# Attention with a sixth of the exp tiles taken from ScalarE to VectorE, heads regrouped by four, and the order set by a planner

## Chip, cores and metric

One core of a Trainium2 chip runs the kernel. The metric is device time in microseconds (us) of one execution, lower is better; medians are over the runs quoted.

## The reference

The block is a sum of an attention and a feed-forward part on the same normalised input, 2048 positions of width 640:

```python
xn = layernorm(x)                                   # x: [1, 2048, 640] bf16
q  = (xn @ wq) split in 32 heads of 20 columns
k, v = xn @ wk, xn @ wv                             # one k and v for all heads
p  = softmax(q k^T / sqrt(20));  o = p v
h  = relu(xn @ w1 + b1) ** 2                        # 1536 wide
out = x + o @ wo + h @ w2 + b2
```

The exp of the scores decides everything: 32 x 2048 x 2048 values. On the chip a tile of them is 128 keys by 512 queries of one head, so there are 2048 tiles (16 key tiles, 4 query chunks, 32 heads).

## The kernel before

Scores are made by TensorE (QK) into two alternating sets of three banks of PSUM (the memory that matmuls write to), one bank for each head of a group of three. ScalarE turns one set into bf16 probabilities with a single exp instruction, and TensorE multiplies them with the values (P-V), accumulating in one bank. Head groups are ten of three and one of two. Everything else on TensorE (query projections, feed-forward, output projection) is cut into small pieces and put between these steps, and where nothing is left, **fillers** are: matmuls with all-zero weights that add 0 to the open P-V sum.

```python
for j in range(NSTEP):                       # 704 steps, cut to the core
    for i in range(HPG):                     # HPG = 3, one bank for each head
        matmul(ps[:, 3*(j%2)+i, :], kT[32*i:32*i+DH, ...], qT[32*i:32*i+DH, ...])   # QK, waits for exp j-2
    activation(out=PT[:, j % NSLOT, 0:nh, :], in_=ps[:, sset:sset+nh, :], func=Exp) # one exp, 2 or 3 banks
    ...
    nfill = 0
    if CFG["enable_fill"] and pvs:
        while busy + COL_NS <= CFG["fill_target_ns"] - (1344.0 - step_ns) + COL_NS / 2:
            nfill += 1                       # fill_target_ns = 1060 of a 1344 ns step
            busy += COL_NS
    emit_pv(k, nfill)                        # fillers, then P-V of an earlier step
    ...
def fillers(k, nh):
    for _ in range(k):
        for jj in range(4):                  # four column groups run together
            matmul(ps[32*jj:32*jj+32, PVB, :], zeros32, kT[:, 0:512], start=False, stop=False)
```

Five dummy matmuls stand ahead of the first QK step. And GpSimd (POOL) clears the pad of the output projection only after the second QK step:

```python
memset(wo_pad, 0.0), waits=[(st_done, 2)]    # on POOL
```

The softmax here doesn't subtract the row's maximum and nothing guards it: scores larger than these inputs give would overflow.

Of the kernel before, what the change touches and what calls it, by code (L numbers as in the profile page):

```python
# [6 lines left out]
F32 = mybir.dt.float32  # L7
ALU = mybir.AluOpType
# [4 lines left out]
HPG = 3  # L13
G = (H + HPG - 1) // HPG
NSLOT = 6
NQS = 4


def NH(g):
    return min(HPG, H - HPG * g)  # L20


GORDER = [0, 1, 2, 3, 4, G - 1, 5, 6, 7, 8, 9]
assert sorted(GORDER) == list(range(G))
SHORT_GI = GORDER.index(G - 1)


def BLK(b):
    qc, gi = divmod(b, G)
    return qc, gi, GORDER[gi]  # L30

SCALE = DH ** -0.5
EPS = 1e-5
NBLK = QC * G
NSTEP = NBLK * KT
# [3 lines left out]
CFG = dict(  # L39
    misc_budget_ns=620.0,  # L40
    fill_target_ns=1060.0,
    enable_fill=True,
    warm_n=22,
    sched_trials=400,
    npro=3,
    npkv=2,
    act_slot_wait=False,
    pre_loop_dummies=5,
    short_fill=1,
    pro_fill=6,  # L50
)
ROW4_NS, COLF_NS, COL_NS, COL320_NS = 390.0, 320.0, 206.0, 140.0
PRO_SCHED = []
# [45 lines left out]

def bass_parallel_sum__grouped_kv_mqa__dense_activation_squared_relu__prompt_kernel(nc, A_x, A_wq, A_wk, A_wv, A_wo, B_x, B_w1, B_b1, B_w2, B_b2, out):  # L100
    es = ExitStack()
    with es:  # L102
# [22 lines left out]
        vx = sb("vx", [128, KT, 32], BF16)  # L125
        qT = sb("qT", [128, NQS, 512], BF16)
        PT = sb("PT", [128, NSLOT, HPG, 512], BF16)
# [11 lines left out]
        out_sb = sb("out_sb", [128, 4, D], BF16)  # L139
        part = sb("part", [128, 4, D], F32)  # L140
        zeros32 = sb("zeros32", [128, 32], BF16)
        scr = sb("scr", [128, 4], F32)
        nk0 = sb("nk0", [128, 2], F32)
        ps = es.enter_context(nc.psum_tensor("ps", [128, 8, 512], F32))

        PVB = 6
        MB = 7
# [4 lines left out]
        junk_src = [PT[:, k, :, :].rearrange("p a n -> p (a n)")[:, 0:D] for k in range(NSLOT)] + \  # L152
# [18 lines left out]
        osem = [newctr(f"osem{i}") for i in range(4)]  # L171
        c_pool = newctr("c_pool")
# [13 lines left out]
        misc_pe = newctr("misc_pe")  # L186
        misc_free = newctr("misc_free")
        act_done = newctr("act_done")
        st_done = newctr("st_done")
        pv_done = newctr("pv_done")  # L190
        pv_evac = newctr("pv_evac")
        c_nrm = newctr("c_nrm")
        norm_done = newctr("norm_done")
        sq_done = newctr("sq_done")
        c_aux = newctr("c_aux")
        c_k0 = newctr("c_k0")

        P = Plan()

        class Unit:  # L200
            def __init__(self, name, groups, n, pe_waits, evac, bank=MB, kind="mm", ncol=4, need_norm=0):
                self.name = name
                self.ncol = ncol
                self.need_norm = need_norm
                self.groups = groups
                self.n = n
                self.pe_waits = pe_waits
                self.evac = evac
                self.bank = bank
                self.kind = kind  # L210
                self.idx = None
                self.next_group = 0
                self.v_done = None

            def cost(self):
                return (COL_NS if self.n >= 500 else COL320_NS)

        unit_seq = []
        last_unit_in_bank = {}

        def emit_unit_group(u):
            k = u.next_group
            L, R = u.groups[k]
            last = (k == len(u.groups) - 1)
            bank = u.bank
            for j in range(u.ncol):
                w = []
                if k == 0 and j == 0:
                    u.idx = len(unit_seq)
                    unit_seq.append(u)  # L230
                    w = list(u.pe_waits() if callable(u.pe_waits) else u.pe_waits)
                    if bank in last_unit_in_bank:
                        w.append((misc_free, last_unit_in_bank[bank] + 1))
                    last_unit_in_bank[bank] = u.idx
                inc = misc_pe if (last and j == u.ncol - 1) else None
                if callable(L):
                    Lj = L(j)
                    m = DH
                else:
                    Lj = L[:, 32 * j:32 * j + 32]  # L240
                    m = 32
                add(P.pe, lambda e, j=j, Lj=Lj, R=R, k=k, last=last, n=u.n, bank=bank, m=m: e.matmul(  # L242
                    ps[32 * j:32 * j + m, bank, 0:n], Lj, R, start=(k == 0), stop=last, tile_position=(0, 32 * j)),
                    waits=w, inc=inc)
            u.next_group += 1
            if last:
                u.v_done = misc_pe.n
                assert u.v_done == u.idx + 1
                u.evac(u)
            return last  # L250

        def emit_unit_all(u):
            while not emit_unit_group(u):
                pass

        qt_units = {}

        def unit_QT(b):
            qc, gi, g = BLK(b)
            groups = [((lambda j, dt=dt: wq_sb[:, dt, DH * (HPG * g + j):DH * (HPG * g + j) + DH]), xnT[:, dt, qc * 512:(qc + 1) * 512]) for dt in range(DT)]  # L260
            pe_waits = [te_wait(st) for st in range(4 * qc, 4 * qc + 4)] + [(wq_sem, 16)]

            def evac(u):
                w = [(misc_pe, u.v_done)]
                if b >= NQS:
                    w.append((st_done, KT * (b - NQS + 1)))
                add(P.dve, lambda e: e.tensor_copy(out=qT[:, b % NQS, :], in_=ps[:, u.bank, :]), waits=w, inc=misc_free)  # L267
            u = Unit(f"QT{b}", groups, 512, pe_waits, evac, ncol=NH(g))
            qt_units[b] = u
            return u  # L270

        ffn_count = [0]
        last_out_unit_of_qc = {}

        def unit_FFN1(qc, f):
            groups = [(w1_sb[:, dt, f * 128:(f + 1) * 128], xnT[:, dt, qc * 512:(qc + 1) * 512]) for dt in range(DT)]
            pe_waits = [te_wait(st) for st in range(4 * qc, 4 * qc + 4)] + [(w1_sem, 16)]

            def evac(u):
                k = ffn_count[0]  # L280
                ffn_count[0] += 1
                w = [(misc_pe, u.v_done), (misc_free, b1_unit[0].idx + 1)]
                if k >= 2:
                    w.append((sq_done, k - 1))
                v_relu = add(P.dve, lambda e: e.tensor_scalar(out=hT_tmp[:, k % 2, :], in0=ps[:, u.bank, :], scalar1=b1col[:, f:f + 1], scalar2=0.0,  # L285
                                                              op0=ALU.add, op1=ALU.max), waits=w, inc=misc_free)
                w2 = [(misc_free, v_relu)]
                if qc >= 2:
                    w2.append((misc_pe, last_out_unit_of_qc[qc - 2]))
                add(P.pool, lambda e: e.tensor_tensor(out=h2T[:, qc % 2, f, :], in0=hT_tmp[:, k % 2, :], in1=hT_tmp[:, k % 2, :], op=ALU.mult),  # L290
                    waits=w2, inc=sq_done)
            return Unit(f"FFN{qc}_{f}", groups, 512, pe_waits, evac)

        b1_unit = [None]

        def unit_B1():
            u = Unit("B1", [None], 0, [(b1_sem, 16), (c_pool, v_ident)], None, kind="b1")
            b1_unit[0] = u
            return u

        def emit_b1_unit(u):
            u.idx = len(unit_seq)
            unit_seq.append(u)
            w = list(u.pe_waits() if callable(u.pe_waits) else u.pe_waits)
            if MB in last_unit_in_bank:
                w.append((misc_free, last_unit_in_bank[MB] + 1))
            last_unit_in_bank[MB] = u.idx
            add(P.pe, lambda e: e.transpose(out=psbf(MB)[:, 0:FT], in_=b1row[:, :], identity=ident[0:FT, 0:FT]), waits=w, inc=misc_pe)
            u.next_group = 1
            u.v_done = misc_pe.n  # L310
            add(P.dve, lambda e: e.tensor_copy(out=b1col[:], in_=psbf(MB)[:, 0:FT]), waits=[(misc_pe, u.v_done)], inc=misc_free)
            return True

        out_dma_count = [0, 0, 0, 0]
        GP1 = 7

        def out_groups(qc, st, half, gs, with_ffn):
            stl = st % 4
            cs = slice(half * 320, half * 320 + 320)
            groups = []  # L320
            if with_ffn:
                for f in range(FT):
                    groups.append((h2T[:, qc % 2, f, stl * 128:(stl + 1) * 128], w2_sb[:, f, cs]))
# [685 lines left out]
```

## Time and profile before

The median was 961.25 us of 3 runs (960.55 to 969.2). The first fence has lines of the profile's page: busy time by engine; busy tenths of ScalarE (ACT) and the granted TensorE clock (PEclk, tenths of full speed) in 40 equal slices of the span; the chain of work that ended last; and two of the costliest groups (busy us, mean ns of one | idle before it).

```profile
span 955.9 us, 26306 instructions
...
PE 851.0 (89%) x12183; PEld 287.5 (30%) x12184; DVE 205.6 (22%) x382; ACT 938.5 (98%) x750; POOL 65.5 (7%) x71
...
ACT  7999999999999999999999999999999999999995
...
PEclk8999999999999999999999999999999999999998
...
ACT 94%; PE 3%; DVE 2%; DMA 1%; issue 0%; ACTq 0%; SPq 0%; DVEq 0%
...
L891 ACT ACTIVATE PT<-ps 128x1536 bf16<-128x1536 f32 (+1 forms) x704 | 918.9, 1767 | 1.4 <-PE ps L888 1.2
...
L814 PE MATMUL ps<-kT,zeros 128*32 128x512 bf16 x2316 | 183.9, 385 | 0.0
```

ScalarE is the bound: 98% busy, 94% of the chain, and the exp group was idle for 1.4 us in all. TensorE (PE) looks busy too (89%), but 183.9 us of that is fillers. The clock is at full speed from start to end. VectorE (DVE) works 22% of the time, so moving exp work there is natural. The second fence is the grouping by shape, which gives the price of an exp instruction: 861.7/640 = 1.346 us for three banks.

```profile
L891 ACT ACTIVATE PT<-ps 128x1536 bf16<-128x1536 f32 x640 | 861.7, 1819 | 1.4 <-PE ps L888 1.2
...
L891 ACT ACTIVATE PT<-ps 128x1024 bf16<-128x1024 f32 x64 | 60.5, 1255 | 0.0
```

In a two-head stretch of the timeline exp instructions follow each other every 0.917 us. So one instruction costs about 0.06 us plus 0.43 us for each 512-column tile. The third fence has busy time in three stretches of 60 us (columns: stretch, length, busy us and instruction count of PE, PEld, DVE, ACT and POOL, then the granted clock, DMA share, GB/s).

```profile
core 0: us, PE busy (x) PEld busy (x) DVE busy (x) ACT busy (x) POOL busy (x), PEclk, DMA share, GB/s
60.00:120.00 60.00, 52.23 (x675) 15.07 (x667) 10.45 (x18) 60.00 (x46) 2.08 (x2) 1.00 0.01 1
180.00:240.00 60.00, 52.08 (x680) 15.05 (x672) 9.18 (x17) 60.00 (x46) 2.08 (x2) 1.00 0.01 2
270.00:330.00 60.00, 54.23 (x836) 19.28 (x832) 11.52 (x20) 60.00 (x46) 2.08 (x2) 1.00 0.01 4
```

### The profile page before, as it was taken

To read this page: it belongs to the slowest core of one execution; us is meant where nothing else is said; L and a number is where in the kernel's file an instruction comes from. 1 tells how busy PE (TensorE), PEld (TensorE's weight loads), DVE (VectorE), ACT (ScalarE), POOL (GpSimd) and SP (SyncE) were. 2 spreads that over 40 slices of the span, in tenths; PEclk is the share of its full clock that TensorE was granted. 3 is DMA by queue.
4 is the path that set the end of the run, shared out by engine and by line. 5 is a ranking of instruction groups with operands and counts; after the bars stand their busy time and mean duration, and the time that the engine had idled before them with its cause. 6 is when DMAs were issued, how large, how long until landed. Compare 5 with 4: busy or idle time off the path is not lost.

```text
span 955.9 us, 26306 instructions
## 1 busy us (share of the span) xinstructions
PE 851.0 (89%) x12183; PEld 287.5 (30%) x12184; DVE 205.6 (22%) x382; ACT 938.5 (98%) x750; POOL 65.5 (7%) x71
## 2 busy tenths in 40 slices
PE   6988889888899998998888998999889999999996
PEld 3322222222233332332233332333223333233332
DVE  6312211112211211211111112121113222112214
ACT  7999999999999999999999999999999999999995
POOL 4300000000000000000000000010001111000000
PEclk8999999999999999999999999999999999999998
DMA  9100000000000000000000000000000000000000
GB/s 311 37 2 1 1 1 1 2 2 1 2 2 8 9 2 1 9 2 8 1 2 9 2 8 2 8 2 9 2 1 2 9 2 8 2 9 2 9 2 29
DMA packets 9412, 12.54 MB, mean 13 GB/s; under 512 B 1751, under 2 KB 8664, under 8 KB 9304
## 3 DMA queue, kind: packets, MB, share of 16 engines
q1 hardware_dynamic: 7992, 10.82, 3.4%
q8 instruction: 96, 1.57, 0.7%
q10 hardware_dynamic: 1312, 0.05, 0.1%
q14 instruction: 12, 0.10, 0.0%
HBM read 8.25 MB, written 2.62 MB: 11 GB/s over the span
## 4 chain that ended last, share of the span: by engine, by line
ACT 94%; PE 3%; DVE 2%; DMA 1%; issue 0%; ACTq 0%; SPq 0%; DVEq 0%
ACT PT L891 94%; PE ps L888 1%; PE ps L242 1%; DMA x_sb<-in_A_x_dram 1%; PE ps L859 1%; PE ps L814 0%; PE ps L521 0%; DVE stats L438 0%; DVE out_sb L379 0%; PE ps L492 0%; DVE big L478 0%; DVE qT L267 0%; ACTq L102 0%; PE ps L529 0%; PE ps L431 0%
## 5 line engine op out<-in xcount | busy, mean ns | idle before, releaser
L891 ACT ACTIVATE PT<-ps 128x1536 bf16<-128x1536 f32 (+1 forms) x704 | 918.9, 1767 | 1.4 <-PE ps L888 1.2
L888 PE MATMUL ps<-qT,kT 20*128 20x512 bf16 x2112 | 275.3, 384 | 66.4 <-ACT PT L891 59.7
L859 PE MATMUL ps<-PT,vx 128*32 128x512 bf16 x2816 | 270.9, 384 | 1.2 <-ACT PT L891 1.2
L814 PE MATMUL ps<-kT,zeros 128*32 128x512 bf16 x2316 | 183.9, 385 | 0.0
L888 PEld LDWEIGHTS ps<-qT,kT 20*128 20x128 bf16 x2112 | 68.4, 90 | 362.6 <-ACT PT L891 349.6
L824 DVE STREAM_TRANSPOSE Tn<-ps 128x512 f32<-128x512 f32 x44 | 31.5, 717 | 449.0 <-PE ps L859 449.0
L859 PEld LDWEIGHTS ps<-PT,vx 128*32 128x32 bf16 x2816 | 70.3, 95 | 108.1 <-issue 77.3
L290 POOL TENSOR_TENSOR big<-hT_tmp 128x512 bf16<-128x512 bf16 x48 | 49.9, 1041 | 716.1 <-DVE hT_tmp L285 716.1
L242 PE MATMUL ps<-w_sb,big 128*32 128x320 bf16 x1536 | 69.1, 300 | 10.8 <-DVE qT L267 9.6
L242 PE MATMUL ps<-xnT,w_sb 128*32 128x512 bf16 x960 | 68.9, 380 | 9.8 <-DVE qT L267 7.6
L242 PE MATMUL ps<-wo_pad,OTn 128*32 128x320 bf16 x1408 | 65.5, 303 | 2.6 <-DVE part L365 2.6
L242 PE MATMUL ps<-xnT,wq_sb 128*20 128x512 bf16 x640 | 62.3, 379 | 1.8 <-DVE qT L267 1.8
L814 PEld LDWEIGHTS ps<-kT,zeros 128*32 128x32 bf16 x2316 | 37.7, 94 | 71.6 <-issue 71.6
L285 DVE TENSOR_SCALAR hT_tmp<-ps,b1col 128x512 bf16<-128x512 f32 x48 | 36.0, 750 | 87.7 <-PE ps L242 87.7
L242 PEld LDWEIGHTS ps<-w_sb,big 128*32 128x32 bf16 x1536 | 39.7, 96 | 32.6 <-issue 18.9
L242 PEld LDWEIGHTS ps<-wo_pad,OTn 128*32 128x32 bf16 x1408 | 38.0, 98 | 18.6 <-DVE OTn L839 2.9
L342 DVE TENSOR_TENSOR out_sb<-ps,x_sb 128x320 bf16<-128x320 f32 x24 | 11.8, 491 | 143.6 <-PE ps L242 143.6
L242 PEld LDWEIGHTS ps<-xnT,w_sb 128*32 128x32 bf16 x960 | 22.7, 95 | 32.7 <-issue 17.2
L267 DVE CAST qT<-ps 128x512 bf16<-128x512 f32 x44 | 29.0, 659 | 12.8 <-PE ps L242 12.8
L839 DVE STREAM_TRANSPOSE OTn<-T 128x512 bf16<-128x512 bf16 x44 | 31.1, 707 | 0.8
L831 DVE TENSOR_TENSOR T<-Tn 96x512 bf16<-96x512 f32 (+1 forms) x44 | 30.2, 687 | 1.5
L242 PEld LDWEIGHTS ps<-xnT,wq_sb 128*20 128x20 bf16 x640 | 21.0, 91 | 18.2 <-issue 2.2
(71 smaller groups left out, 135.0 us busy)
## 6 DMA issues: line engine op xcount, KB each, us to landing
w_sb<-in_B_w_dram SPq DMA_DIRECT2D x2, 1920.0 KB, 10.6
out_dram<-out_sb SPq DMA_DIRECT2D x16, 160.0 KB, 1.8
x_sb<-in_A_x_dram SPq DMA_DIRECT2D x3, 640.0 KB, 7.2
wq_sb<-in_A_wq_dram SPq DMA_DIRECT2D x1, 800.0 KB, 10.1
x_sb<-in_A_x_dram SPq DMA_DIRECT2D x2, 320.0 KB, 3.6
wo_pad<-in_A_wo_dram SPq DMA_DIRECT2D x2, 275.0 KB
wo_pad<-in_A_wo_dram SPq DMA_DIRECT2D x1, 250.0 KB
wk_c<-in_A_wk_dram ACTq DMA_DIRECT2D x1, 25.0 KB, 3.4
```

The source lines that it names most:

```text
L242: add(P.pe, lambda e, j=j, Lj=Lj, R=R, k=k, last=last, n=u.n, bank=bank, m=m: e.matmul(ps[32 * j:32 * j + m, bank, 0:n], Lj, R, start=(k = ...
L267: add(P.dve, lambda e: e.tensor_copy(out=qT[:, b % NQS, :], in_=ps[:, u.bank, :]), waits=w, inc=misc_free)
L285: v_relu = add(P.dve, lambda e: e.tensor_scalar(out=hT_tmp[:, k % 2, :], in0=ps[:, u.bank, :], scalar1=b1col[:, f:f + 1], scalar2=0.0, op0 ...
L290: add(P.pool, lambda e: e.tensor_tensor(out=h2T[:, qc % 2, f, :], in0=hT_tmp[:, k % 2, :], in1=hT_tmp[:, k % 2, :], op=ALU.mult), waits=w2 ...
L342: v = add(P.dve, lambda e: e.tensor_tensor(out=out_sb[:, slot, cs], in0=ps[:, u.bank, 0:320], in1=x_sb[:, st, cs], op=ALU.add), waits=w, i ...
L814: add(P.pe, lambda e, jj=jj: e.matmul(ps[32 * jj:32 * jj + 32, PVB, :], zeros32[:, :], kT[:, 0:512], start=False, stop=False, tile_positio ...
L824: add(P.dve, lambda e: e.transpose(out=Tn[:, a, :], in_=ps[:, PVB, :]), waits=w, inc=pv_evac)
L831: st8["v2"] = add(P.dve, lambda e: e.tensor_tensor(out=T2[0:pp, a, :].rearrange("p (c d) -> p c d", d=32), in0=Tn[0:pp, a, :].rearrange("p ...
L839: add(P.dve, lambda e: e.transpose(out=OTn[:, qc % 2, g, :], in_=T2[:, a, :]), waits=w3, inc=norm_done)
L859: add(P.pe, lambda e, i=i, t=t, hs=hs: e.matmul(ps[32 * i:32 * i + 32, PVB, :], vx[:, t, :], PT[:, j % NSLOT, hs, :], start=(t == 0), stop ...
L888: add(P.pe, lambda e, i=i, t=t, b=b, sset=sset: e.matmul(ps[:, sset + i, :], kT[32 * i:32 * i + DH, t * 128:(t + 1) * 128], qT[32 * i:32 * ...
L891: add(P.act, lambda e, j=j, nh=nh, sset=sset: e.activation(out=PT[:, j % NSLOT, 0:nh, :], in_=ps[:, sset:sset + nh, :], func=AF.Exp, bias= ...
```

## The change

Its intent: give 84 of the 512 (head group, query chunk, key tile) sets of four tiles to VectorE, so that ScalarE has 1712 tiles instead of 2048. VectorE has to build the exp from bit patterns. One step scales the score and writes it as a 16-bit integer: read as bf16, these bits `L` are 2^e times a mantissa u in [1, 2). Two mask steps give `W` (the exponent with a constant mantissa) and `U` = u; two multiplies give `T` = L u u. TensorE then sums three P-V products with the values scaled by 1, 0.5 and 0.164, which is 2^e (u + 0.98 + 0.164 u^3), close to a constant times 2^e 2^u. One bank is VectorE's; ScalarE keeps two sets, of three and of two banks. The second multiply of every other set runs on POOL.

Heads are in 8 groups of four, so P-V and normalisation passes drop from 44 to 32. The order of all instructions comes from a list scheduler in the kernel that has a duration for each instruction and puts the real work of each engine into its free time. The fillers are gone. So are the five dummies and the wait of the memset. The diff, cut to its core (marked ...):

```diff
-HPG = 3
-G = (H + HPG - 1) // HPG
+HPG = 4
+G = H // HPG
...
+ACT_BANKS = ((0, 1, 2), (3, 4))
+DBANKS = (5,)
+T2POOL = (0, 1)
...
-            add(P.pool, lambda e: e.memset(wo_pad[:], 0.0), waits=[(st_done, 2)], inc=c_pool)
+            add(P.pool, lambda e: e.memset(wo_pad[:], 0.0), waits=[], inc=c_pool)
...
-        pe_dummies(CFG["pre_loop_dummies"])
-        for j in range(NSTEP):
...          # and the fillers, with all of the fixed step loop
+            d1 = dv(... e.tensor_scalar(out=lbuf[:, a, cs].bitcast(U16), in0=ps[:, bank, :], scalar1=XA, scalar2=XB, op0=ALU.mult, op1=ALU.add) ...)
+            s["wop"] = [dv(... e.tensor_scalar(out=W.bitcast(U16), in0=L.bitcast(U16), scalar1=0xFF80, scalar2=124, op0=ALU.bitwise_and, op1=ALU.bitwise_or) ...)]
+            s["uop"] = dv(... e.tensor_scalar(out=ubuf.bitcast(U16), in0=L.bitcast(U16), scalar1=0x7F, scalar2=0x3F80, op0=ALU.bitwise_and, op1=ALU.bitwise_or) ...)
+            s["t1"] = [dv(... e.tensor_tensor(out=T, in0=L, in1=ubuf, op=ALU.mult) ...)]
+            # second multiply: two halves on POOL in every other set, else on VectorE
+        while True:            # the planner: of all engines' ready work, take what can start first
...
```

## The prediction

It was written before the changed kernel had run.

> **What bounds it now.** ScalarE's exp. The page gives ACT 98% busy (938.5 of a 955.9 us span); the chain of waits puts 94% of the span on the exp line, and the exp group was idle only 1.4 us. By shape: 640 activations of 128x1536 (861.7 us, so 1.346 us each at full rate) and 64 of 128x1024; in a two-head stretch of the timeline one starts every 0.917 us. That is about 0.06 us per instruction plus 0.43 us per 512-column tile, 2048 tiles. About 37 us lie outside (first exp at 26.5 us; an 11 us tail). PE is 89% busy, but 184 us of that is filler matmuls on zeros; DVE only 22%, POOL 7%.
>
> **What the change does, by counted instructions.** 84 of 512 (block, key tile) sets, 336 of 2048 tiles, leave ScalarE. It keeps 1712 tiles in 342 three-tile and 343 two-tile steps: 342 x 1.344 + 343 x 0.917 = 774 us instead of 919. Gain 145 us.
>
> DVE gains, for each set: four PSUM-to-integer steps (128x512 from PSUM took 0.66 to 0.75 us in this trace), two mask operations on 128x2048 16-bit, one multiply, and in half of the sets a second multiply. The trace has none of the big ones; the Trainium skill, "VectorE: DVE Perf Modes", section "Side-by-side: where the cycles go for N=2048 bf16", gives about 0.69 us in 4x mode and 1.22 us in 2x (nothing here shows it yet). Estimate: 336 x 0.70 + 168 x 0.69 + 84 x 1.22 + 42 x 1.22 = 505 us. Groups of four need 32 instead of 44 normalisations and query casts (-35 us). DVE: about 675 us, over 80% of the new span. POOL gains 84 multiplies of 1024 columns, about 2.08 us each (twice its 512-column 1.041 us): +175 us.
>
> PE loses all 2316 fillers and a quarter of the P-V passes, gains 336 x 3 matmuls for the three terms. Estimate from strides in the timeline (0.32 us a QK step, 0.22 us four P-V columns): about 570 us, not the bound.
>
> **Critical path.** If exp stays saturated: 961 - 145 = 816 us. I do not expect that. DVE is now near full, in order, with one PSUM bank for its score tiles, whose matmul stands in PE's queue between ScalarE's QK steps: when DVE is late, PE blocks and ScalarE starves. DVE's two-port and two-input operations and POOL's multiplies exclude each other (Trainium skill, "SBUF — State Buffer", section "SBUF: two separate sides": an exclusive lock), so a 2.1 us POOL multiply can hold DVE. I allow 4 to 5% of stalls, about 35 us.
>
> **Predicted: 850 us, 8 in 10 between 824 and 892.** Faster by over 2%: 0.93; within 2%: 0.03; slower: 0.04.
>
> **What would show it.** Exp busy about 775 us, ACT 91 to 95% of the span, with 30 to 50 us idle released by PE's QK, behind PE waits on DVE's PSUM step. DVE near 80%, mask operations near 0.69 us, multiplies near 1.2 us, POOL multiplies near 2.1 us. PE near 70%, clock above 0.97.
>
> **What would make it wrong.** Mask operations not in 4x mode (1x would be over 2 us, +250 us on DVE: about 950 us or worse); lock waits that stretch DVE or POOL multiplies well beyond their durations; a PE clock that drops without fillers; or stalls under 1% (about 822 us).

## The result

The changed kernel took 884.65 us in the median of 4 runs (881.98 to 886.22), in the same job the kernel before 960.9. The ratio is 0.9188 (95% interval 0.9139 to 0.9238). Ratios here are the mean time of one kernel's fast runs over that of the other's in the same rounds, so they are not quite the ratios of the medians. It is faster, within the predicted range, but 35 us slower than the number predicted, and 69 us above the 816 us of a saturated ScalarE. Its page, with the lines that answer to those of before:

```profile
span 882.4 us, 20648 instructions
...
PE 790.4 (90%) x9319; PEld 239.7 (27%) x9319; DVE 658.4 (75%) x942; ACT 809.1 (92%) x732; POOL 251.3 (28%) x162
...
ACT  7599998998889999999889989999998999999895
...
PEclk8689987655569999977559999986576999965799
...
PE 48%; ACT 42%; DVE 6%; issue 1%; DVEq 0%
...
L840 ACT ACTIVATE PT<-ps 128x1536 bf16<-128x1536 f32 (+1 forms) x685 | 788.6, 1265 | 57.1 <-PE ps L533 54.0
...
L956 DVE TENSOR_SCALAR x_sb<-ps 128x512 uint16<-128x512 f32 x336 | 230.5, 686 | 140.8 <-PE ps L533 138.8
L972 POOL TENSOR_TENSOR tbuf<-tbuf,x_sb 128x1024 bf16<-128x1024 bf16 x84 | 178.8, 2151 | 435.5 <-DVE tbuf L967 435.5
...
L967 DVE TENSOR_TENSOR tbuf<-x_sb 128x2048 bf16<-128x2048 bf16 x84 | 103.7, 1235 | 1.4
...
L963 DVE TENSOR_SCALAR x_sb<-x_sb 128x2048 uint16<-128x2048 uint16 x84 | 69.3, 825 | 1.4
L965 DVE TENSOR_SCALAR x_sb<-x_sb 128x2048 uint16<-128x2048 uint16 x84 | 62.1, 740 | 0.0
```

Two things stand out. First, PEclk: 6 and 5 stand in long rows where before all were 9, and the mean clock is 0.814 (before 0.993). Second, the chain is now split between PE (48%) and ACT (42%), and exp waited 57.1 us, 54.0 of it for PE. VectorE's steps cost about what was foreseen: 0.686 us for a score tile, 1.235 us for a multiply, 0.74 and 0.825 us for the masks, 2.15 us for POOL's half multiply. The same three stretches as before:

```profile
core 0: us, PE busy (x) PEld busy (x) DVE busy (x) ACT busy (x) POOL busy (x), PEclk, DMA share, GB/s
60.00:120.00 60.00, 54.65 (x686) 16.01 (x690) 52.81 (x73) 59.44 (x53) 22.93 (x17) 1.00 0.01 2
180.00:240.00 60.00, 54.86 (x376) 10.97 (x376) 39.95 (x54) 51.59 (x45) 13.02 (x8) 0.53 0.00 1
270.00:330.00 60.00, 57.60 (x924) 21.69 (x924) 53.84 (x73) 59.72 (x54) 17.38 (x11) 1.00 0.06 18
```

At full clock (first and third row) ScalarE is busy 59.4 and 59.7 of 60 us and finishes 53 and 54 exp steps. At a clock of 0.53 it finishes 45. The lines of the timeline there, and of the same time in the kernel before (start, length, instructions), show why:

```profile
200.37 0.62 PE L533 MATMUL ps<-PT,vx 128*32 128x512 bf16 x4
200.77 1.07 PE L533 MATMUL ps<-xnT,w_sb 128*32 128x512 bf16 x8
...
204.14 0.61 PE L533 MATMUL ps<-qT,kT 20*128 20x512 bf16 x3
204.68 0.62 PE L533 MATMUL ps<-PT,vx 128*32 128x512 bf16 x4
```

```profile
201.40 0.39 PE L859 MATMUL ps<-PT,vx 128*32 128x512 bf16 x4
201.98 0.39 PE L888 MATMUL ps<-qT,kT 20*128 20x512 bf16 x3 [0.19 <-ACT PT L891]
202.30 0.61 PE L814 MATMUL ps<-kT,zeros 128*32 128x512 bf16 x8
```

Starts count here, since ends overlap. In the changed kernel four P-V matmuls take 0.40 us (200.37 to 200.77) and a QK step of three matmuls 0.54 (204.14 to 204.68). Before, a QK step of three took 0.32 (201.98 to 202.30), and in a full-clock stretch of the changed kernel four P-V matmuls take 0.22 (271.04 to 271.26). At about half speed PE can no longer refill the banks in the time of an exp: from 200 to 210 us PE was busy for 10.00 of 10 us, and exp was idle for 2.8 us waiting for it.

The start is also later. In the kernel before, the first exp began at 26.5 us; now at 31.4 us (the first line is of the kernel before, the second of the changed one):

```profile
26.54 2.97 ACT L891 ACTIVATE PT<-ps 128x1536 bf16<-128x1536 f32 x2 [1.01 <-PE ps L888]
```

```profile
31.44 2.37 ACT L840 ACTIVATE PT<-ps 128x1536 bf16<-128x1536 f32 x2 [5.38 <-PE ps L533]
```

The timeline of VectorE and POOL in the changed kernel:

```profile
23.46 5.97 DVE L301 TENSOR_SCALAR big<-x_sb,rstd,nmr 128x640 bf16<-128x640 bf16 x3
```

```profile
24.52 4.36 POOL L391 MEMSET wo_pad<- 128x5120 bf16 x1
```

Three normalising steps took 5.97 us together; one of them, by the per-tile view, 5.234 us, where the others took about 0.45. POOL ran a normalising step of its own from 23.53 (1.05 us) and right after it the memset, which lost its wait in the change, from 24.52 to 28.88. The long VectorE step spans both.

### The profile page after: what moved, and what is told of

Read it like the earlier page. It is cut to its first block, busy times and chain, and to the rows that moved or that the text cites. A ratio compares the mean times of both kernels' runs of the same rounds, so it can differ in the third digit from the quotient of the medians.

```text
span 882.4 us, 20648 instructions
## 1 busy us (share of the span) xinstructions
PE 790.4 (90%) x9319; PEld 239.7 (27%) x9319; DVE 658.4 (75%) x942; ACT 809.1 (92%) x732; POOL 251.3 (28%) x162
## 4 chain that ended last, share of the span: by engine, by line
PE 48%; ACT 42%; DVE 6%; issue 1%; DVEq 0%
PE ps L533 48%; ACT PT L840 42%; DVE x_sb L956 1%; DVE hT_tmp L652 1%; DVE Tn L890 1%; DVE qT L635 1%; DVE T L892 0%; DVE x_sb L965 0%; PE ps L581 0%; DVE out_sb L715 0%; DVE out_sb L1132 0%; DVE x_sb L963 0%; DVE part L734 0%; DVE OTn L896 0%; DVE tbuf L967 0%
## 5 line engine op out<-in xcount | busy, mean ns | idle before, releaser
L840 ACT ACTIVATE PT<-ps 128x1536 bf16<-128x1536 f32 (+1 forms) x685 | 788.6, 1265 | 57.1 <-PE ps L533 54.0
L533 PE MATMUL ps<-qT,kT 20*128 20x512 bf16 x2048 | 332.9, 458 | 63.2 <-ACT PT L840 55.2
L956 DVE TENSOR_SCALAR x_sb<-ps 128x512 uint16<-128x512 f32 x336 | 230.5, 686 | 140.8 <-PE ps L533 138.8
L972 POOL TENSOR_TENSOR tbuf<-tbuf,x_sb 128x1024 bf16<-128x1024 bf16 x84 | 178.8, 2151 | 435.5 <-DVE tbuf L967 435.5
L533 PE MATMUL ps<-PT,vx 128*32 128x512 bf16 x1712 | 201.6, 462 | 2.4 <-DVE Tn L890 2.4
L967 DVE TENSOR_TENSOR tbuf<-x_sb 128x2048 bf16<-128x2048 bf16 x84 | 103.7, 1235 | 1.4
L963 DVE TENSOR_SCALAR x_sb<-x_sb 128x2048 uint16<-128x2048 uint16 x84 | 69.3, 825 | 1.4
L965 DVE TENSOR_SCALAR x_sb<-x_sb 128x2048 uint16<-128x2048 uint16 x84 | 62.1, 740 | 0.0
L974 DVE TENSOR_TENSOR tbuf<-tbuf,x_sb 128x2048 bf16<-128x2048 bf16 x42 | 51.7, 1232 | 0.2
L533 PE MATMUL ps<-tbuf,vxc 128*32 128x512 bf16 x336 | 39.2, 456 | 0.3 <-POOL tbuf L972 0.2
L533 PE MATMUL ps<-x_sb,vxh 128*32 128x512 bf16 x336 | 38.8, 452 | 0.0
```

The lines of the kernel that those rows point to most:

```text
L533: return lambda e: e.matmul(out_, l, r, start=start, stop=stop, tile_position=tp)
L840: return Op(f"ACT{st_['j']}", "ACT", 0.064 + 0.4267 * n, [lambda e: e.activation(out=PT[:, s0:s0 + n, :], in_=ps[:, b0:b0 + n, :], func=AF ...
L956: d1 = dv(f"D1_{n}_{i}", 0.66, lambda e: e.tensor_scalar(out=lbuf[:, a, cs].bitcast(U16), in0=ps[:, bank, :], scalar1=XA, scalar2=XB, op0= ...
L963: s["wop"] = [dv(f"W{n}", 0.65, lambda e: e.tensor_scalar(out=W.bitcast(U16), in0=L.bitcast(U16), scalar1=0xFF80, scalar2=124, op0=ALU.bit ...
L965: s["uop"] = dv(f"U{n}", 0.65, lambda e: e.tensor_scalar(out=ubuf.bitcast(U16), in0=L.bitcast(U16), scalar1=0x7F, scalar2=0x3F80, op0=ALU. ...
L967: s["t1"] = [dv(f"T1_{n}", 1.17, lambda e: e.tensor_tensor(out=T, in0=L, in1=ubuf, op=ALU.mult), [s["uop"]] + ([("pv", old, 2)] if old els ...
```

## Experiments

The theories at the start. **A:** the time above 816 us comes from the TensorE clock, which falls where PE's work is thin, because the fillers are gone. **B:** it comes from VectorE and POOL being late (exclusive lock, one bank), as the prediction had it. **C:** PE's queue is too full for its order. All kernels gave correct results. The base of each ratio is the kernel before, run in the same job.

### e1_fill: fillers back

```diff
+ gap = o.start - seq["PE"][i_ - 1].fin            # after the plan is made; its order is not touched
+ if gap >= 0.2: nfill_of[id(o)] = min(9, int(gap / 0.215))
+ matmul(ps[32*jj:32*jj+32, PVB, 0:512], zeros32, kT[:, 0:512], start=False, stop=False)   # x4 for each
```

> The changed kernel with every real instruction in its place and 670 groups of four 512-column zero matmuls put into PE's planned gaps of 0.2 us or more (about 144 us of PE time). Theory A (the lost time is the TensorE clock, which falls to half where PE's work is thin): granted clock from 0.81 to 0.97 or more, exp idle from 57 us to under 15 us, time 815 to 832 us. Rival B (VectorE and POOL lateness: exclusive lock, single bank for VectorE's score tiles): the clock may rise, but exp idle stays at 40 us or more and the time stays above 865 us. Rival C (PE's queue is too full for its order): more PE work makes it slower than 885 us.

Measured: 845.45 us (844.48 to 846.9), ratio 0.879 (0.8753 to 0.8827), clock 0.991.

```profile
span 842.8 us, 26009 instructions
...
PE 813.9 (97%) x11999; PEld 279.4 (33%) x11999; DVE 659.3 (78%) x943; ACT 808.5 (96%) x732; POOL 251.1 (30%) x162
...
PEclk8899999999999999999999999999999999999999
...
PE 80%; ACT 9%; DVE 5%; POOL 2%; issue 0%; DVEq 0%
...
L843 ACT ACTIVATE PT<-ps 128x1536 bf16<-128x1536 f32 (+1 forms) x685 | 788.1, 1286 | 17.4 <-PE ps L536 13.8
...
L1191 PE MATMUL ps<-kT,zeros 128*32 128x512 bf16 x2680 | 202.4, 380 | 0.0
```

```profile
180.00:240.00 60.00, 58.50 (x781) 17.34 (x783) 45.41 (x66) 59.70 (x53) 14.74 (x8) 1.00 0.01 2
```

39 us come back by adding 202 us of useless work to PE. The thin stretch now has 53 exp steps at full clock, not 45. B and C predicted no gain or a loss. But A's number was missed too (815 to 832), and exp still waited 17.4 us where under 15 was expected; PE is now busy 97%, and the chain is 80% PE.

### e2_tiny: the same instructions, without the work

```diff
- matmul(ps[32*jj:32*jj+32, PVB, 0:512], zeros32, kT[:, 0:512], ...)
+ matmul(ps[32*jj:32*jj+32, PVB, 0:16],  zeros32, kT[:, 0:16],  ...)
```

> The same instructions in the same places as e1_fill, but each zero matmul moves 16 columns instead of 512. Theory A: the clock stays near 0.8 and the time within 2% of the changed kernel (875 to 895 us), although the instruction count and order equal e1_fill's. If instead some effect of having more instructions in the queue were the cure, it would be as fast as e1_fill.

Measured: 883.99 us (878.41 to 892.54; ratio 0.917 of the fast runs), clock 0.822. In the thin stretch:

```profile
180.00:240.00 60.00, 58.05 (x644) 14.77 (x642) 37.65 (x52) 51.09 (x44) 13.65 (x7) 0.50 0.01 1
```

The median is of all four runs; 892.54 counts as slow, and the other three are 878.41 to 886.11. That is as the changed kernel. What helps is the time PE spends streaming, not the presence or place of instructions.

### e3_before_nofill: the kernel before, without its fillers

```diff
-    enable_fill=True,
+    enable_fill=False,
-    short_fill=1,
+    short_fill=0,
```

> The kernel before without its 2316 zero matmuls. Theory A: PE's remaining work (about 585 us of 919) is thinner than in the changed kernel, the clock falls to 0.5 to 0.7, exp is starved in those stretches and the time is 4% or more above before (over 1000 us). Rival B: the fillers never mattered; the clock may fall, but the time stays within 1% of before (952 to 970 us).

Measured: 1038.94 us (1035.41 to 1044.63), ratio 1.0805 (1.0742 to 1.0868), clock 0.764.

```profile
60.00:120.00 60.00, 51.78 (x363) 11.07 (x363) 8.51 (x14) 56.07 (x43) 2.08 (x2) 0.59 0.00 1
180.00:240.00 60.00, 51.25 (x385) 11.37 (x381) 10.87 (x18) 54.42 (x41) 3.12 (x3) 0.61 0.01 1
```

43 and 41 exp steps in 60 us instead of 46. The fillers were worth 8% to the kernel before; the change dropped them, and e1 shows what that cost there.

### e4_noD_fill: grouping and order alone

```diff
-ACT_BANKS = ((0, 1, 2), (3, 4))
+ACT_BANKS = ((0, 1, 2), (3, 4, 5))
-PTR = 20
+PTR = 24
+            return None        # first line of make_dqk: no set is given to VectorE; fillers as in e1_fill
```

> Only the regrouping by four and the new order, no tile on VectorE: all 2048 exp tiles on ScalarE in three-tile steps with two sets of three banks, with zero matmuls in PE's gaps. 683 steps x 1.344 us = 918 us plus about 37 us outside: 950 to 965 us, same as before (theories A and B alike). If the grouping or the order were worth something by themselves, it would be below 940 us.

Measured: 973.41 us (972.48 to 974.94), ratio 1.0122: above the expected span. Its trace has the clock at 0.50 and 0.67 from 30 to 50 us; e9 takes this up.

### e5_fill_head: the memset's wait

```diff
-            add(P.pool, lambda e: e.memset(wo_pad[:], 0.0), waits=[], inc=c_pool)
+            add(P.pool, lambda e: e.memset(wo_pad[:], 0.0), waits=[done[f"XN{st}"] for st in range(ST)], inc=c_pool)
```

> e1_fill plus one wait: POOL's memset of the output-projection pad waits for the last normalised input tile, as it in effect did before the change (there it waited for the second QK step). In the changed kernel's trace one of VectorE's normalising steps took 5.2 us instead of 0.45 while that 4.4 us memset ran, and the first exp came at 31.4 us instead of 26.5. Theory D (the memset holds VectorE[...]): no VectorE normalising step above 1.2 us, first exp at 26.5 to 28 us, time 4 to 9 us below e1_fill's 845 (836 to 841). If the late first exp has another cause, within 2 us of e1_fill.

Measured: 840.41 us (839.62 to 845.22), ratio 0.8751 (0.8705 to 0.8797), 5 us below e1_fill. The two ran in different jobs and their intervals overlap, so the 5 us are likely, not certain. The normalising steps and the memset in its timeline:

```profile
25.34 1.60 DVE L304 TENSOR_SCALAR big<-x_sb,rstd,nmr 128x640 bf16<-128x640 bf16 x3 [0.26 <-DVE nmr L297]
```

```profile
27.06 4.36 POOL L394 MEMSET wo_pad<- 128x5120 bf16 x1 [1.01 <-DVE big L304]
```

Three steps now take 1.60 us. In this profiled execution (845.22 us, the slowest of the four) the first exp nevertheless came only at 29.9 us, which was not expected. The clock was low in the start of that execution. In e6 and e7, which have the same wait, the first exp came at 26.7 and 26.6 us; in e1, without it, at 32.0.

### e6_dens75 and e7_dens62: fewer fillers

```diff
-                if gap >= 0.2: nfill_of[id(o)] = min(9, int(gap / 0.215))
+                # one more filler only while it leaves 0.1 us of the gap, and only while PE's planned
+                # work (with fillers) of the last 4 us is under 75% (e7: 62%)
```

> e5 with only 368 groups of zero matmuls instead of 670: one is put in only where PE's planned work of the last 4 us is under 75%. Theory E (in e1_fill the zero matmuls, placed also where PE is dense anyway, delay QK steps: exp cost 788 us instead of 774 and idle 17): clock stays above 0.97, exp busy 780 us or less, time 822 to 834 us. Against it: if those delays come from the real work in PE's queue, time equals e5's within 3 us.

Measured: 827.69 us (826.83 to 834.34), ratio 0.8623 (0.8572 to 0.8675). The clocks of its runs were 0.98, 0.992, 0.998 and 0.998, and the times follow them: 834.34, 828.51, 826.83, 826.87.

```profile
span 832.6 us, 23596 instructions
...
L843 ACT ACTIVATE PT<-ps 128x1536 bf16<-128x1536 f32 (+1 forms) x685 | 781.7, 1319 | 14.5 <-PE ps L536 12.0
```

Theory E's numbers hold: too many fillers also cost time. That QK steps queue behind them is the likely reason, but argued only: between the profiled runs of e5 and e6 exp's busy time fell from 788.7 to 781.7 us, and its idle time hardly (15.0 to 14.5). The edit also changed the least gap that gets a filler and took away the limit of nine.

> As e6 with the aim at 62% (224 groups). It asks how much PE work keeps the clock. In the changed kernel the clock fell where planned PE work was about 50% of a 10 us stretch and stayed where it was 75 to 80%. If the edge lies between 50 and 62%, the clock stays above 0.97 and the time is at or a little below e6's; if it lies above 62%, the clock falls in the thin stretches (0.85 to 0.95) and the time is 840 us or more.

Measured: 845.26 us with a wide spread (835.23 to 867.39; ratio of the fast runs 0.8756), clocks 0.957 to 0.978 in the fast runs. The single 867.39 us run counts as slow; its mean clock was 0.914. The fast runs are 835.23 to 846.55 us. So 62% of planned work is not safe and 75% nearly is. No sharper edge was measured. The changed kernel fits this: with the planner's list laid over its trace exp by exp, planned PE work is 44 to 69% in the 10 us stretches after 50 us that had a clock of 0.50, and about 75% or more in all but two of those at 1.00.

### e8_head_only: the memset's wait alone

The edit is that of e5, on the changed kernel.

> The changed kernel with only the memset's wait, no zero matmuls. Theory D: first exp 3 to 5 us earlier, and the clock does not fall in the first 20 us after it, since PE no longer stands idle for 5 us; time 873 to 881 us instead of 884. The stretches of half clock later on stay: mean clock 0.80 to 0.85.

Measured: 881.34 us (875.45 to 888.35), ratio 0.9169 (0.9101 to 0.9238). The first exp came at 27.6 us, 3.8 us earlier, and the clock was 0.85 or more from 30 to 60 us where the changed kernel had 0.50 for 20 us. The wait alone does not secure that clock: e6's profiled run, which has it too, shows 0.59 and 0.73 from 30 to 50 us. But in the total this is not told apart from the changed kernel: the intervals overlap almost wholly. With the clock free to fall later, 3 us drown in the spread.

### e9_noD_dens: grouping and order alone, with start and fillers mended

The edits of e4, e5 and e6 together.

> e4 (grouping by four and the new order alone, every tile on ScalarE) with the memset's wait of e5 and the sparser zero matmuls of e6. e4 was 973 us where 918 + 37 = 955 was expected; its trace shows the late first exp and a half clock from 30 to 50 us, as in the changed kernel. If those two, which e5 and e6 mended, were all of the 12 us, it comes to 953 to 964 us: grouping and order are worth nothing by themselves. If it stays above 968 us, the order itself costs something.

Measured: 963.43 us (962.08 to 964.23), ratio 1.0033 (1.0013 to 1.0053). Exp is busy 919.0 us and idle 6.0. Grouping by four and the new order show no gain by themselves; against e6, which differs in the moved tiles, the gain is all in the tiles moved off ScalarE. Start and fillers were mended together, so how they share e4's 10 us is not known.

### e10_t2_dve and e11_t2_pool: who does the second multiply

```diff
-T2POOL = (0, 1)
+T2POOL = (0,)     # e10: VectorE always;   e11: T2POOL = (1,), POOL always
```

Both on top of e6. The planner runs anew in each, so places of instructions and fillers differ a little (351 and 371 groups instead of 368); VectorE has 84 sets in all three.

> e6 with every second multiply of the polynomial on VectorE: POOL loses its 84 multiplies (180 us), VectorE gains 42 of 1.23 us. Rival B (exclusive lock between POOL and VectorE limits the kernel): faster than e6 by 5 us or more, about 815 to 822. Rival B2 (VectorE's load limits it): slower by 10 us or more. If neither limits once the clock is held: within 5 us of e6's 827 to 828.

Measured: 821.47 us (819.38 to 823.06), ratio 0.8555 (0.8535 to 0.8574).

```profile
span 819.8 us, 23436 instructions
...
ACT 70%; PE 21%; DVE 6%; issue 1%; DMA 1%; SPq 0%; DVEq 0%
...
L843 ACT ACTIVATE PT<-ps 128x1536 bf16<-128x1536 f32 (+1 forms) x685 | 777.1, 1367 | 5.4 <-PE ps L536 4.7
...
L966 DVE TENSOR_SCALAR x_sb<-x_sb 128x2048 uint16<-128x2048 uint16 x84 | 63.3, 754 | 1.6
L968 DVE TENSOR_SCALAR x_sb<-x_sb 128x2048 uint16<-128x2048 uint16 x84 | 58.6, 698 | 0.0
```

> e6 with every second multiply on POOL (168 instead of 84 multiplies of 2.15 us, 52 us less on VectorE). Rival B: slower than e6 by 10 us or more, with VectorE's mask steps longer than 0.9 us in the mean. Rival B2: faster by 5 us or more. Neither: within 5 us of e6.

Measured: 831.99 us (828.12 to 834.04), ratio 0.8656 (0.8632 to 0.868). One of its mask steps took 0.879 us in the mean.

The medians stand in the order e10, e6, e11, but part of this is the clock: e10's runs had 0.991 to 0.999, e11's 0.985 to 0.995. At nearly equal clocks e10 and e6 have 819.38 (0.999) and 826.83 (0.998), e10 and e11 in the same job 821.42 (0.995) and 828.12 (0.995), but e6 and e11 828.51 (0.992) and 828.31 (0.994). So taking POOL's multiplies away gains about 5 to 7 us, and doubling them costs nothing that can be told apart; e11 is within 5 us of e6, the "neither" of its expectation. B holds for a small part at most, and since the planner ran anew, the new places of instructions are a rival that was not tested. The first mask step, 0.825 us in the changed kernel, takes 0.754 in e10. VectorE's higher load (684.4 us, 83%) does no harm.

e10 is the fastest kernel here: 7% below the changed kernel, 14% below the one before.

### e12_best: more fillers and the dummies

```diff
+        pe_dummies(CFG["pre_loop_dummies"])     # ahead of the loop, on top of e6; fillers to 82% instead of 75%
```

> e6 with the aim raised from 75% to 82% of planned PE work (432 groups) and with the five dummy matmuls ahead of the first QK step put back, which the kernel before had and the change dropped. If what is left of the clock's dips (30 to 50 us, and short ones later) is what separates e6's runs (826.8 to 834.3 us at mean clocks of 0.998 to 0.980): clock 0.99 or more in all runs, time 822 to 829 us, spread under 4 us. If more zero matmuls cost more than they save: 829 to 835 us.

Measured: 830.3 us (826.8 to 836.31), ratio 0.8654 (0.8622 to 0.8685), clocks 0.981 to 0.995. A miss: no better than e6, and the spread is 9.5 us. Two things were changed at once. The dips of the clock that are left between e6's runs are not cured by a higher aim. Their cause stays open.

## Why the prediction was right or wrong

**Right: the bound and the gain at full clock.** 342 x 1.344 + 343 x 0.917 = 774 us of exp was the base; e10 has 777.1 us busy and 5.4 idle, and 821.47 us against the 816 of the sum. e9 shows that nothing else in the change gains.

**Right: the cost on VectorE and POOL.** 675 us was estimated for VectorE, 658.4 measured; 0.70 for a score tile, 0.686 measured; 1.22 for a multiply, 1.235 measured; 2.08 for POOL's, 2.15 measured. Masks were put at 0.69 and took 0.74 and 0.825: the rest may be contention, as e10 with its 0.698 and 0.754 suggests; in e11, with twice the multiplies on POOL, they took 0.719 and 0.879.

**Wrong: the step "The granted clock above 0.97", and with it the cause of the stalls.** The prediction said of PE: "about 570 us, not the bound", and let the fillers go at no cost. It listed "a PE clock that drops without fillers" only among the things that would make it wrong. It had the number at hand: 184 us of matmuls on zeros in an already tuned kernel, with no use for the result, must do something. The sum 35 us for stalls measured 69. In the order in which they were taken away, starting from 884.65 us: fillers 39 us (e1), the memset's wait 5 (e5), fillers only where PE is thin 13 (e6), POOL's multiplies 6 (e10); 5 us remain above 816. These parts are differences of medians, most of them across jobs, and they depend on the order: without fillers, the wait alone (e8) shows no sure gain.

**Wrong: "when DVE is late, PE blocks and ScalarE starves".** In the changed kernel's table of waits, PE's weight loads wait for VectorE's PSUM step 7.5 us in total, at most 0.6 at once, while VectorE waits 138.8 us for PE. The queue is blocked the other way round. No run gave VectorE a second bank, so this rests on the table alone. Exp's idle time of 30 to 50 us "released by PE's QK" was nearly right in size (57.1), but its cause was PE's speed.

**Right by luck in part: the time.** 884.65 lies inside 824 to 892 because the allowance for one loss covered another.

**Not foreseen: the memset.** The diff shows the dropped wait in plain sight, and the prediction names the very lock that makes it matter, but only for POOL's multiplies. By e5 it costs about 5 us.

**Open.** How the clock is decided (the measure, the edge, why a cold stretch lasts), and the dips left in e6 and e12.

## What to carry to other kernels

Work that looks useless in a tuned kernel is a question to ask before it is deleted: here zero matmuls worth 8% held the TensorE clock. When a change thins an engine whose clock depends on its load, look at the granted clock first, stretch by stretch, and refill only where planned work is thin, since too many fillers delay the real work. Every wait that a diff removes is a change of its own; ask what now runs at the same time and what the two share.

## What the Trainium skill lacked or had wrong

- "TensorE: Matmul & The Clock Gate", section "HAM oscillation — how this bites in real kernels", warns of idle gaps over about 3.4 us. In the changed kernel no wait of a matmul after the start was longer than 1.4 us, and the clock fell all the same, to 0.50 for tens of us. The page's next section, "A second HAM failure mode: psum-queue depth-cycling", does report a clock that swings from frequent short idle times, which is nearer. The section "Part 1: The HAM clock gate (the "warmup" mystery)" describes half and full speed, and that agrees: most stretches of 10 us have 0.50 or 1.00. What the page lacks is how much work is enough: here fillers up to 75% of planned PE time over 4 us held the clock at 0.98 to 0.998, 62% did not (0.957 to 0.978 in the fast runs).
- "Part 1: The HAM clock gate (the "warmup" mystery)" says that about 3.4 us of sustained work bring full speed. From 180 to 240 us PE was busy 54.86 of 60 us and the clock stayed at 0.53 (from 200 to 210 us 10.00 of 10, at 0.50). So busy time as the profile shows it did not tell the clock here; that matmuls of 20 or 32 rows or columns, run side by side, count for less is a guess.
- No page says that matmuls with all-zero weights hold the clock (0.991 in e1) or that 16-column ones do not (0.822 in e2).
- "SBUF — State Buffer", section "SBUF: two separate sides", has the exclusive lock between VectorE and GpSimd. It agrees, and it is worth adding that a plain GpSimd memset is enough: a 0.45 us VectorE step took 5.23 us beside a GpSimd step of 1.05 us and the memset of 4.36 us that followed it at once.
- "VectorE: DVE Perf Modes", section "Side-by-side: where the cycles go for N=2048 bf16", gives 693 and 1224 ns for the 4x and 2x modes. That agrees: 0.698 and 0.754 us for the two 16-bit mask steps in e10, 1.235 us for a multiply in the changed kernel. The page does not name masks on 16-bit integers among the fast ones.
